# Attention with two expert layers on one core: 64-row tile first, raw float32 scores for it, loads spread over three queues

## The chip, the cores and the metric

One core of a Trainium2 chip runs the whole program. TensorE (PE) multiplies, VectorE (DVE), ScalarE (ACT) and GpSimd (POOL) do the rest, and the sync engine (SP) issues transfers; ACT and POOL can issue transfers too. The metric is the device time of one execution in microseconds, the median of several runs.

## The reference

Two batches of 8 heads, 576 positions, 64 numbers per head. A learned bias depends on the positions alone. The result goes through two layers of experts.

```python
scores = q @ k.T / sqrt(64)
bias = relu(x @ w1 + b1) @ w2        # x = log1p(|i - j|) / log1p(max(i, 1)), 32 hidden, 8 heads
attn = softmax(scores + bias);  y = attn @ v
y = sum_e p[:, e] * (relu(y @ w1[e]) @ w2[e])    # 4 experts, given probabilities
y = sum_e P[:, e] * (relu(y @ w1[e]) @ w2[e])    # 8 experts, P from 8 Sinkhorn rounds
```

## The kernel before

**Attention** takes the first 200 us or so. Rows of the scores are cut into tiles t = 0 to 3 of 128 rows for each batch, and a tile t = 4 that holds the last 64 rows of both batches. Heads go in pairs p = 0 to 3. A unit is one (t, p, b), or one (4, p): 36 units, in the order of `tps_` (t = 0, 4, 1, 2, 3). Units are numbered 0 to 35, and k is the pass of the loop that starts unit k.

A pass issues, in this order, for the units in flight: the scores of unit k (`emit_S`, TensorE, into two PSUM tiles tagged `sc`), for which q and k were first split into a rounded part and a rest (`prep_q`, `prep_k`: three products instead of one); score plus bias with the row minimum of the negative (`emit_max`, DVE, one instruction for each head); `emit_recip2` of unit k-1; `emit_x` of unit k-4 (DVE: divides the product with V and writes `rows`); the two exponentials (`emit_exp`, ACT); the transposes of unit k-2 (`emit_T`, TensorE) and their copies out (`emit_evac`, ACT); one more group of the bias; and the product with V of unit k-3 (`emit_P`, TensorE, into `po`). Every engine runs its own instructions in the order in which they were issued; there is no scheduler.

**The bias** of 16 rows is a group, 36 in all. Hidden values come from DVE or ACT (`emit_hid`), TensorE multiplies (`bps`), ACT copies out into one of three staging slots (`bsts`, two instructions), and the sync queue stores to memory (`bd`). `load_bias` reads a unit pair's bias back (`bt`, two buffers); it waits until the groups of its tile are stored. For tile 4 it takes four transfers. Tile 4 has another head pair in each unit, the other tiles in every second unit. Eleven groups are made before the loop, one in each pass after it.

**Queues.** All transfers before are on the sync queue in one order: q (`qr`), k (`kr`), V, the bias both ways, later the weights.

**The rest.** From unit 15 on, finished rows are cut up for the first expert layer (`pieces`: ACT copies, then DVE), one part in a pass. The expert layers follow, with TensorE busy nearly throughout.

Of the kernel before, what the change touches and what calls it, by code (L numbers as in the profile page):

```python
# [9 lines left out]
F32 = mybir.dt.float32  # L10
# [38 lines left out]
def attn_moe_moe(ctx: ExitStack, tc: tile.TileContext, pack, keep, rel, qT, kT, vT, w, out):  # L49
# [126 lines left out]
    def attention(moe):  # L176
# [19 lines left out]
        def load_v(p):  # L196
            sy.dma_start(out=V[p][:, 0:4, :], in_=vT[p, 0:512].rearrange("(j p) x -> p j x", p=128))
            gp.memset(V[p][:, 4, :], 0.0)
            for h in range(2):
                to, of = (x.rearrange("p (b h d) -> p h b d", b=2, h=2)[:, h] for x in (V[p][:, 4, :], vT[p, 512:576]))  # L200
                sy.dma_start(out=to[64 * h:64 * h + 64], in_=of)

        bdram = [dram.tile([H, (128 if t < 4 else 64) + 1, W], F32, name=f"bd{t}") for t in range(5)]


        tps_ = [(t, p) for t in (0, 4, 1, 2, 3) for p in range(4)]
        units = [(t, p, b) for t, p in tps_ for b in range(2 if t < 4 else 1)]
# [3 lines left out]

        def load_k(p, b):
            i = 2 * p + b
            r = xa.tile([128, 1280], F32, tag=f"x0{XA[i % 4]}", name=f"kr{p}{b}")[:, 0:S]
            for h in range(2):
                sy.dma_start(out=r[64 * h:64 * h + 64], in_=kT[p, b, 0:64, S * h:S * h + S])
            rawk[p, b] = r

        def prep_k(p, b, hi):
            r = rawk.pop((p, b))  # L220
            kk[p, b] = ata.tile([128, 2, S], F32R, name=f"kk{p}{b}")
            h = kk[p, b][:, 0, :]
            if hi is sc:
                sc.activation(out=h, in_=r, func=AF.Copy)
            else:
                ve.tensor_copy(h, r)
            ve.tensor_tensor(out=kk[p, b][:, 1, :], in0=r, in1=h.bitcast(F32), op=ALU.subtract)

        def load_q(t, p):
            r = ata.tile([128, 256], F32, tag="qraw", name=f"qr{t}{p}", bufs=3)  # L230
            for h in range(2):
                sy.dma_start(
                    out=r[64 * h:64 * h + 64].rearrange("p (b c) -> p b c", b=2),
                    in_=qT[t, p, 0:64].rearrange("p (b h c) -> p h b c", b=2, h=2)[:, h],
                )
            rawq[t, p] = r

        def prep_q(t, p):
            r = rawq.pop((t, p))
# [30 lines left out]
        taken = {}  # L270
        MORE = 56

# [64 lines left out]
        def emit_S(u):  # L337
            t, p, b = units[u]
            o = [ps.tile([128, 2, 512], F32, tag="sc", name=f"sc{u}{h}", bufs=2) for h in range(2)]

            todo = [(x, y, bb) for x, y in ((0, 1), (1, 0), (0, 0)) for bb in ([b] if t < 4 else [0, 1])]
            for j in range(2):
                for i, (x, y, bb) in enumerate(todo):
                    for h in range(2):
                        d = slice(64 * h, 64 * h + 64)
                        pe.matmul(  # L346
                            out=o[h][:, j, 0:288],
                            lhsT=qq[t, p][d, x, 128 * bb:128 * bb + 128],
                            rhs=kk[p, bb][d, y, 288 * j:288 * j + 288],
                            start=i == 0,  # L350
                            stop=i == len(todo) - 1,
                        )
# [134 lines left out]

        FIRST = 8
        hids(8, (1, 5))
        for g in range(FIRST):  # L490
            groups(1)
            if g == 0:
                prep_q(*tps_[0])
            if g == 1:
                prep_k(*kq[0], ve)
            hids(4, (1,))
            if g == 3:
                load_k(*kq[3])
            if g == 4:
                prep_k(*kq[1], ve)  # L500
            if g == 6:
                load_k(*kq[4])
                load_q(*tps_[2])

        load_bias(*tps_[0])
        load_bias(*tps_[1])
        load_k(*kq[5])
        load_q(*tps_[3])
        prep_q(*tps_[1])
        prep_k(*kq[2], sc)  # L510
        for _ in range(3):
            groups(1)
            hids(4)
        prep_k(*kq[3], sc)

        ti, work, first_split = 0, [], None
        for k in range(U + 3):
            first = False
            if k < U:
                t, p, b = units[k]  # L520
                first = b == 0
                if first:
                    ti = tps_.index((t, p))
# [30 lines left out]
            hids(2)  # L554
            if k >= 3 and k - 3 < U:
# [428 lines left out]
```

## Time and profile before

| | us |
|---|---|
| median of 3 runs (1386.51 to 1392.95) | 1389.74 |
| the profiled execution | 1390.56 |
| its span, first to last instruction | 1388.6 |
| start of the first score reduction | 29.8 |
| start of that of unit 12 | 95.3 |
| start of that of unit 35 (the last) | 198.8 |

Times in the views count from the span's start. "Idle before, releaser" in square brackets is how long an engine stood still before an instruction and what ended it. PE busy is modelled. Matmuls of float32 leave two records each, of the rounded type one.

### The profile page before, as it was taken

The page shows a single profiled execution, that of the slowest core. Times are in us where ns is not written, and L with a number is a line of the kernel's source. Part 1 is how long each engine was busy: PE and PEld are TensorE (multiplying, and loading weights), DVE is VectorE, ACT ScalarE, POOL GpSimd, SP SyncE. Part 2 cuts the span into 40 slices and gives each one's busy share as a digit, 9 for nine tenths or more (in the row PEclk, how much of TensorE's full clock was granted, in tenths as well). Part 3 has the DMA queues.
Part 4 walks back from the last instruction along what each step waited for, and adds up shares of the span by engine and source line. Part 5 has one row for each costly group of instructions (what it writes and reads, how often), then busy time and mean ns, then how long its engine had stood idle before and what let it go on. Part 6 is the DMA issues. An engine that isn't in the chain of part 4 may idle for free.

```text
span 1388.6 us, 22435 instructions
## 1 busy us (share of the span) xinstructions
PE 1343.7 (97%) x8763; PEld 1172.5 (84%) x8763; DVE 794.9 (57%) x1786; ACT 507.1 (37%) x1208; POOL 390.4 (28%) x391
## 2 busy tenths in 40 slices
PE   7889988999999999999999999999999999999998
PEld 3666676899899898889888898898998988988987
DVE  7768778456464473584585463563554744735643
ACT  6768774233142241344242241331321422413311
POOL 0111134044062160153061160350430612604400
PEclk9999999999999999999999999999999999999999
DMA  7765521111021020011021030020110200301110
GB/s 211 197 175 145 156 66 61 31 58 65 0 85 38 1 95 27 1 61 61 1 91 31 3 96 24 31 92 1 62 61 1 92 31 24 96 4 33 59 39 31
DMA packets 42169, 84.67 MB, mean 61 GB/s; under 512 B 10320, under 2 KB 17744, under 8 KB 42064
## 3 DMA queue, kind: packets, MB, share of 16 engines
q1 hardware_dynamic: 42064, 83.24, 19.6%
q8 instruction: 69, 1.13, 0.3%
q14 instruction: 36, 0.29, 0.1%
HBM read 69.97 MB, written 13.25 MB: 60 GB/s over the span
## 4 chain that ended last, share of the span: by engine, by line
PE 84%; DVE 8%; ACT 3%; DMA 2%; issue 2%; SPq 1%; POOL 0%; DVEq 0%; ACTq 0%; POOLq 0%
PE y L726 42%; PE B L647 16%; PE C L647 10%; PE A L647 10%; DVE s L364 2%; PE po L435 2%; PE sc L346 1%; ACT s L377 1%; DMA bt<-bd 1%; DMA bd<-bsts 1%; PE bps L297 1%; PE tp L409 1%; ACT bsts L326 1%; ACT at L418 1%; DVE wt L158 0%
## 5 line engine op out<-in xcount | busy, mean ns | idle before, releaser
L726 PE MATMUL y<-gb,h 128*128 128x512 f32 x2592 | 717.3, 397 | 0.0
L726 PEld LDWEIGHTS y<-gb,h 128*128 128x128 f32 x2592 | 454.1, 189 | 57.0 <-issue 0.2
L162 POOL TENSOR_TENSOR gb<-rawb,gb 128x512 fp32r<-128x512 f32 x94 | 126.1, 1354 | 644.1 <-ACT gb L161 611.6
L655 DVE TENSOR_TENSOR u<-B,s 128x320 f32<-128x320 f32 (+1 forms) x192 | 87.7, 457 | 309.9 <-PE B L647 309.9
L658 ACT ACTIVATE h<-c 128x320 fp32r<-128x320 f32 (+1 forms) x288 | 119.9, 439 | 390.6 <-DVE c L655 389.2
L661 DVE SCALAR_TENSOR_TENSOR h<-c,h 128x320 fp32r<-128x320 f32 (+1 forms) x288 | 172.0, 614 | 48.3 <-ACT h L658 43.8
L655 DVE TENSOR_TENSOR c<-C,u 128x320 f32<-128x320 f32 (+1 forms) x192 | 87.5, 456 | 60.9 <-PE C L647 57.5
L162 POOL TENSOR_TENSOR ga<-rawa,ga 128x512 fp32r<-128x512 f32 x94 | 120.9, 1305 | 4.5 <-ACT ga L161 4.5
L162 POOL TENSOR_TENSOR ga<-wt,ga 128x512 fp32r<-128x512 f32 x94 | 106.0, 1147 | 35.5 <-ACT ga L161 17.9
L669 ACT ACTIVATE s<-A 128x320 f32<-128x320 f32 (+1 forms) x96 | 39.4, 411 | 177.5 <-PE A L647 177.4
L658 ACT ACTIVATE h<-A 128x320 fp32r<-128x320 f32 (+1 forms) x96 | 39.0, 406 | 147.0 <-PE A L647 146.7
L655 DVE TENSOR_TENSOR c<-B,s 128x320 f32<-128x320 f32 (+1 forms) x96 | 44.0, 458 | 81.5 <-PE B L647 80.2
L161 ACT ACTIVATE gb<-rawb 128x512 fp32r<-128x512 f32 x96 | 60.1, 627 | 80.7 <-DMA rawb<-in_w 80.7
L377 ACT ACTIVATE s<-s,stat 128x576 f32<-128x576 f32 x72 | 55.4, 769 | 42.4 <-DVE stat L364 41.6
L435 PEld LDWEIGHTS po<-at,V 128*64 128x64 f32 x800 | 39.3, 137 | 33.9 <-DVE rows L445 32.7
L647 PE MATMUL A<-x20A,ga 128*128 128x320 f32 x384 | 66.9, 309 | 0.0
L647 PE MATMUL B<-x20S,ga 128*128 128x320 f32 x384 | 66.8, 309 | 0.0
L647 PE MATMUL C<-x20S,ga 128*128 128x320 f32 x384 | 66.7, 309 | 0.0
L647 PEld LDWEIGHTS B<-x20S,ga 128*128 128x128 f32 x384 | 61.6, 188 | 5.8
L647 PEld LDWEIGHTS A<-x20A,ga 128*128 128x128 f32 x384 | 61.5, 188 | 5.7
L647 PEld LDWEIGHTS C<-x20S,ga 128*128 128x128 f32 x384 | 61.3, 188 | 5.8
L435 PE MATMUL po<-at,V 128*64 128x128 f32 (+1 forms) x800 | 47.5, 267 | 16.3 <-DVE rows L445 16.3
(167 smaller groups left out, 1905.9 us busy)
## 6 DMA issues: line engine op xcount, KB each, us to landing
rawa<-in_w SPq DMA_DIRECT2D x48, 512.0 KB, 4.0
rawb<-in_w SPq DMA_DIRECT2D x48, 512.0 KB, 4.9
bd<-bsts SPq DMA_DIRECT2D x36, 295.5 KB, 3.4
bt<-bd SPq DMA_DIRECT2D x16, 512.0 KB, 4.4
qr<-in_qT SPq DMA_DIRECT2D x40, 64.0 KB, 3.2
kr<-in_kT SPq DMA_DIRECT2D x16, 144.0 KB, 3.3
V<-in_vT SPq DMA_DIRECT2D x4, 512.0 KB, 4.7
bt<-bd SPq DMA_DIRECT2D x8, 256.0 KB, 4.1
```

Source lines behind the costliest of these rows:

```text
L161: sc.activation(out=z(0), in_=src, func=AF.Copy)
L162: lo.tensor_tensor(out=z(1), in0=src, in1=z(0).bitcast(F32), op=ALU.subtract)
L297: pe.matmul(out=o[32 * q:32 * q + 32, j, 0:n], lhsT=w2n, rhs=hid[g, q][:, n * j:n * j + n], start=True, stop=True,)
L364: ve.tensor_tensor_reduce(out=s.rearrange("p (a j) -> p a j", a=2), in0=scps.pop((u, h))[:, :, 0:288], in1=bt[t, p][:, S * h:S * h + S].re ...
L377: sc.activation(out=s, in_=s, func=AF.Exp, scale=-1.0, bias=stat[u][:, h:h + 1], accum_out=stat[u][:, 2 + h:3 + h],)
L435: pe.matmul(out=o[64 * h:64 * h + 64, c0:c0 + n], lhsT=V[p][:, j, col:col + D], rhs=rhs, start=j == 0, stop=j == 4,)
L647: pe.matmul(out=ban[o], lhsT=a, rhs=x[:, z, k, :], start=not more and i == 0, stop=i == 5, skip_group_check=more,)
L655: ve.tensor_tensor(out=t[o], in0=ban[a], in1=t[b], op=ALU.add)
L658: sc.activation(out=h[f][:, 0, half, :], in_=src, func=AF.Relu)
L661: ve.scalar_tensor_tensor(out=h[f][:, 1, half, :], in0=src, scalar=0.0, in1=h[f][:, 0, half, :].bitcast(F32), op0=ALU.max, op1=ALU.subtract,)
L669: sc.activation(out=t["s1"], in_=ban["A"], func=AF.Copy)
L726: pe.matmul(out=self.y[t], lhsT=a, rhs=x, start=g == 0 and f == 0 and i == 0, stop=g == NP - 1 and f == 1 and i == 2,)
```

## The change

- `tps_` begins with tile 4: its four units are 0 to 3, tile 0's are 4 to 11. From unit 12 on the units are the same. The groups are made in the order 32 to 35, then 0 to 31; nine stand before the loop.
- Tile 4's scores are taken in float32 from raw q and k: 8 matmuls of 64 rows by 64 columns by 288 instead of 24.
- k of a head pair comes as one tile for both batches, all four from ACT's queue at the start. `prep_k` stands in passes 1 to 8, all with ACT.
- q and V come through GpSimd's queue, q three pairs ahead instead of four.
- `emit_x` stands before `emit_S` and `emit_max` of its pass, no longer behind them.
- Six matmuls on ones stand behind the scores in passes 0 to 2. Pass 4 makes two groups; pass 3 makes four more hidden rows.

```diff
-            sy.dma_start(out=V[p][:, 0:4, :], in_=vT[p, 0:512].rearrange("(j p) x -> p j x", p=128))
+            gp.dma_start(out=V[p][:, 0:4, :], in_=vT[p, 0:512].rearrange("(j p) x -> p j x", p=128))
...
-        tps_ = [(t, p) for t in (0, 4, 1, 2, 3) for p in range(4)]
+        tps_ = [(t, p) for t in (4, 0, 1, 2, 3) for p in range(4)]
-        def load_k(p, b):
+        def load_k(p, eng):
+            for b in range(2):
+                rawk[p, b] = r[:, S * b:S * b + S]
             for h in range(2):
-                sy.dma_start(out=r[64 * h:64 * h + 64], in_=kT[p, b, 0:64, S * h:S * h + S])
+                eng.dma_start(
+                    out=r[64 * h:64 * h + 64, 0:2 * S].rearrange("d (b s) -> d b s", b=2),
+                    in_=kT[p, :, 0:64, S * h:S * h + S].rearrange("b d s -> d b s"),
+                )
-            r = ata.tile([128, 256], F32, tag="qraw", name=f"qr{t}{p}", bufs=3)
+            r = ata.tile([128, 256], F32, tag="qraw", name=f"qr{t}{p}", bufs=4)
             for h in range(2):
-                sy.dma_start(
+                gp.dma_start(
...
-            todo = [(x, y, bb) for x, y in ((0, 1), (1, 0), (0, 0)) for bb in ([b] if t < 4 else [0, 1])]
+            todo = [(b, 0, 128, x, y) for x, y in ((0, 1), (1, 0), (0, 0))] if t < 4 else [(0, 0, 64, None, None), (1, 64, 64, None, None)]
...
+                        a, m = (qq[t, p][:, x], kk[p, bb][:, y]) if t < 4 else (rawq[t, p], rawk[p, bb])
                         pe.matmul(
-                            out=o[h][:, j, 0:288],
+                            out=o[h][c:c + n, j, 0:288],
...
+        def busy(n):
+            for _ in range(n):
+                pe.matmul(out=po_all[:, 0, 0:128], lhsT=ones, rhs=ones, start=True, stop=True)
...
+        for p in range(4):
+            load_k(p, sc)
+        for i in range(3):
+            load_q(*tps_[i])
-        order = list(range(8)) + list(range(32, NGR)) + list(range(8, 32))
+        order = list(range(32, NGR)) + list(range(32))
-        FIRST = 8
+        FIRST = 4
...
+        load_bias(*tps_[0])
+        load_v(0)
+        for g in range(5):
+            groups(1)
+            hids(4, (1,))
             if g == 0:
+                load_bias(*tps_[1])
+            if g == 2:
+                load_v(1)
...
+                if k >= 4:
+                    emit_x(k - 4)
                 emit_S(k)
+                if k < 3:
+                    busy(6)
                 emit_max(k)
                 if k > 0:
                     emit_recip2(k - 1)
-                if k >= 4:
-                    emit_x(k - 4)
...
-            groups(1)
+            groups(2 if k == 4 else 1)
...
-            if k < 4:
-                prep_k(*kq[k + 4], sc)
+            if 0 < k < 9:
+                prep_k(*kq[k - 1], sc)
             if k < 2:
-                load_k(*kq[k + 6])
-            if k < 8 and k % 2 == 0:
-                load_v(k // 2)
+                load_v(k + 2)
```

The order on three queues, in places that matter below.

DVE around the fifth unit before (`kk31` is the rest of k for pair 3, batch 1; `s4` the reduced scores of unit 4; `rows0` what `emit_x` writes):

```order
L387 RECIPROCAL stat2_467<-stat2_467 128x2
L283 TENSOR_SCALAR hids_109<-T_99,b1psi_98 128x384 x2
L227 TENSOR_TENSOR kk31_583<-kr31_448,kk31_583 128x576
L364 ISA s4_603,stat4_602<-sc40_586,bt02_442 128x576
L364 ISA stat4_602 128x1
L364 ISA s4_603,stat4_602<-sc41_587,bt02_442 128x576
L364 ISA stat4_602 128x1
L387 RECIPROCAL stat3_534<-stat3_534 128x2
L445 TENSOR_TENSOR rows0_76<-po_95,at02_488 128x128
```

and around the seventh unit now:

```order
L286 TENSOR_SCALAR hidS3_156<-T_99,b1psi_98 128x368 x2
L286 TENSOR_SCALAR hidS4_157<-T_99,b1psi_98 128x368 x2
L230 TENSOR_TENSOR kk20_742<-kr2_130,kk20_742 128x576
L449 TENSOR_TENSOR rows4_80<-po_95,at22_610 128x128
L368 ISA s6_763,stat6_762<-sc60_746,bt01_566 128x576
L368 ISA stat6_762 128x1
L368 ISA s6_763,stat6_762<-sc61_747,bt01_566 128x576
L368 ISA stat6_762 128x1
L391 RECIPROCAL stat5_681<-stat5_681 128x2
L286 TENSOR_SCALAR hids_109<-T_99,b1psi_98 128x352 x4
```

A `kk` row stands ahead of the reduction in both, now with `rows4`, the `emit_x` of unit 2, between them; before, `rows0` stood behind the reduction. Such a `kk` row stands ahead of the reduction of units 2 to 9 now, and stood ahead of units 1 to 4 in the loop before.

The sync queue from the store of group 32 on before (`bd` is a store of a bias group, `bt` a load):

```order
L329 DMA bd4_108<-bsts_110 16x8x591 x4
L232 DMA qr40_393<-in_qT 64x2x128 x2
L216 DMA kr30_399<-in_kT 64x576 x2
L197 DMA V0_100<-in_vT 128x4x256
L201 DMA V0_100<-in_vT 64x2x64 x2
L329 DMA bd1_105<-bsts_110 16x8x591
L255 DMA bt02_442<-bd0_104 128x2x512
L256 DMA bt02_442<-bd0_104 128x2x64
L216 DMA kr31_448<-in_kT 64x576 x2
L329 DMA bd1_105<-bsts_110 16x8x591
L232 DMA qr41_508<-in_qT 64x2x128 x2
L197 DMA V1_101<-in_vT 128x4x256
```

and now:

```order
L332 DMA bd4_108<-bsts_110 16x8x591 x4
L258 DMA bt40_224<-bd4_108 64x2x512
L259 DMA bt40_224<-bd4_108 64x2x64
L258 DMA bt40_224<-bd4_108 64x2x512
L259 DMA bt40_224<-bd4_108 64x2x64
L332 DMA bd0_104<-bsts_110 16x8x591
L258 DMA bt41_249<-bd4_108 64x2x512
L259 DMA bt41_249<-bd4_108 64x2x64
L258 DMA bt41_249<-bd4_108 64x2x512
L259 DMA bt41_249<-bd4_108 64x2x64
L332 DMA bd0_104<-bsts_110 16x8x591 x5
L258 DMA bt42_356<-bd4_108 64x2x512
```

The loads of q, k and V have gone from between the stores and the loads of the bias. Tile 4's loads, four for each unit, stand ahead of the store of tile 0's first group, and the second unit's ahead of that of the next five.

GpSimd's own order in the first passes before (`stat` readies the denominators of a unit, `spread` writes their reciprocals out wide):

```order
L383 TENSOR_SCALAR stat0_367<-stat0_367 128x2
L198 MEMSET V0_100 128x256
L389 COPY spread0_425<-stat0_367 128x128
L383 TENSOR_SCALAR stat1_420<-stat1_420 128x2
L389 COPY spread1_472<-stat1_420 128x128
L383 TENSOR_SCALAR stat2_467<-stat2_467 128x2
```

and now:

```order
L387 TENSOR_SCALAR stat0_334<-stat0_334 128x2
L235 DMA qr43_353<-in_qT 64x2x128 x2
L197 DMA V2_102<-in_vT 128x4x256
L198 MEMSET V2_102 128x256
L201 DMA V2_102<-in_vT 64x2x64 x2
L393 COPY spread0_386<-stat0_334 128x128
L387 TENSOR_SCALAR stat1_381<-stat1_381 128x2
L235 DMA qr00_403<-in_qT 64x2x128 x2
L197 DMA V3_103<-in_vT 128x4x256
L198 MEMSET V3_103 128x256
L201 DMA V3_103<-in_vT 64x2x64 x2
L393 COPY spread1_441<-stat1_381 128x128
L387 TENSOR_SCALAR stat2_436<-stat2_436 128x2
```

Five transfers stand between `stat0` and `spread0`, and five more between `stat1` and `spread1`.

## Rows read from the trace of the kernel before

**Rows 1.** The page: span, and busy time of each engine.

```profile
span 1388.6 us, 22435 instructions
PE 1343.7 (97%) x8763; PEld 1172.5 (84%) x8763; DVE 794.9 (57%) x1786; ACT 507.1 (37%) x1208; POOL 390.4 (28%) x391
```

**Rows 2.** Busy time of PE, PEld, DVE, ACT, POOL by stretch; then clock, DMA.

```profile
0.00:95.30 95.30, 79.35 (x790) 52.38 (x790) 66.39 (x192) 64.40 (x141) 9.18 (x32) 0.95 0.73 200
95.30:201.80 106.50, 93.78 (x1143) 72.76 (x1143) 84.60 (x271) 84.31 (x223) 25.72 (x63) 1.00 0.47 131
```

**Rows 3.** DVE in order of time (start, us, instruction): first score reduction of nine units.

```profile
29.77 0.76 DVE L364 CUSTOM_DVE_ANT_0 s<-sc,bt 128x576 f32<-128x576 f32 x1 [1.60 <-DMA bt<-bd]
...
41.29 0.75 DVE L364 CUSTOM_DVE_ANT_0 s<-sc,bt 128x576 f32<-128x576 f32 x1
...
53.05 0.75 DVE L364 CUSTOM_DVE_ANT_0 s<-sc,bt 128x576 f32<-128x576 f32 x1
...
57.30 0.76 DVE L364 CUSTOM_DVE_ANT_0 s<-sc,bt 128x576 f32<-128x576 f32 x1 [0.47 <-PE sc L346]
...
76.69 0.76 DVE L364 CUSTOM_DVE_ANT_0 s<-sc,bt 128x576 f32<-128x576 f32 x1 [0.95 <-PE sc L398]
...
95.31 0.76 DVE L364 CUSTOM_DVE_ANT_0 s<-sc,bt 128x576 f32<-128x576 f32 x1 [2.86 <-DMA bt<-bd]
...
156.10 0.75 DVE L364 CUSTOM_DVE_ANT_0 s<-sc,bt 128x576 f32<-128x576 f32 x1
...
160.18 0.76 DVE L364 CUSTOM_DVE_ANT_0 s<-sc,bt 128x576 f32<-128x576 f32 x1
...
190.24 0.76 DVE L364 CUSTOM_DVE_ANT_0 s<-sc,bt 128x576 f32<-128x576 f32 x1 [1.06 <-PE sc L346]
```

**Rows 4.** The chain of waits in order of time, 0 to 110 us (start, us, what).

```profile
1.15 3.39 DMA T<-in_rel
...
22.38 3.24 DMA bd<-bsts
...
42.09 0.70 ACT s L377
...
45.89 0.58 ACT kk L224
46.49 0.76 DVE kk L227
...
84.77 3.68 DMA bt<-bd
```

**Rows 5.** The chain of waits, 150 to 200 us.

```profile
161.70 0.20 DVE rows L445
...
161.94 1.31 PE po L435 x20
163.26 1.03 PE sc L346 x12
```

**Rows 6.** ScalarE (ACT) in order of time, first 10 us.

```profile
0.71 1.28 ACT L285 ACT_TABLE_LOAD   x1 [0.71 <-PEq L973]
5.12 1.43 ACT L285 ACTIVATE hids<-T,b1psi 128x576 f32<-128x576 f32 x2 [3.13 <-DVE T L466]
7.82 1.05 ACT L326 ACTIVATE bsts<-bps,cst 128x576 f32<-128x576 f32 x2 [1.27 <-PE bps L297]
...
9.40 1.04 ACT L326 ACTIVATE bsts<-bps,cst 128x560 f32<-128x560 f32 x2
```

**Rows 7.** The sync queue (SPq), in order of time.

```profile
1.62 1.31 SPq L232 DMA_DIRECT2D qr<-in_qT  x2
...
62.15 0.60 SPq L255 DMA_DIRECT2D bt<-bd  x1
```

**Rows 8.** Who waited for whom (us, times, longest), 0 to 210 us.

```profile
PE po L435 <- DVE rows L445: 16.3, 18, 2.2
```

**Rows 9.** The page's costliest groups: one GpSimd (POOL) operation.

```profile
L162 POOL TENSOR_TENSOR gb<-rawb,gb 128x512 fp32r<-128x512 f32 x94 | 126.1, 1354 | 644.1 <-ACT gb L161 611.6
```

More of the change, by code (lines that the diff above doesn't have):

```diff
@@ L200, in load_v @@
                 to, of = (x.rearrange("p (b h d) -> p h b d", b=2, h=2)[:, h] for x in (V[p][:, 4, :], vT[p, 512:576]))
-                sy.dma_start(out=to[64 * h:64 * h + 64], in_=of)
+                gp.dma_start(out=to[64 * h:64 * h + 64], in_=of)
         bdram = [dram.tile([H, (128 if t < 4 else 64) + 1, W], F32, name=f"bd{t}") for t in range(5)]
-        tps_ = [(t, p) for t in (0, 4, 1, 2, 3) for p in range(4)]
+        tps_ = [(t, p) for t in (4, 0, 1, 2, 3) for p in range(4)]
         units = [(t, p, b) for t, p in tps_ for b in range(2 if t < 4 else 1)]
@@ L209, in attention @@
         kk, qq, bt, rawk, rawq = {}, {}, {}, {}, {}
-        def load_k(p, b):
-            i = 2 * p + b
-            r = xa.tile([128, 1280], F32, tag=f"x0{XA[i % 4]}", name=f"kr{p}{b}")[:, 0:S]
+        def load_k(p, eng):
+            r = xa.tile([128, 1280], F32, tag=f"x0{XA[p]}", name=f"kr{p}")
+            for b in range(2):
+                rawk[p, b] = r[:, S * b:S * b + S]
             for h in range(2):
-                sy.dma_start(out=r[64 * h:64 * h + 64], in_=kT[p, b, 0:64, S * h:S * h + S])
-            rawk[p, b] = r
+                eng.dma_start(
+                    out=r[64 * h:64 * h + 64, 0:2 * S].rearrange("d (b s) -> d b s", b=2),
+                    in_=kT[p, :, 0:64, S * h:S * h + S].rearrange("b d s -> d b s"),
+                )
         def prep_k(p, b, hi):
-            r = rawk.pop((p, b))
+            r = rawk[p, b]
             kk[p, b] = ata.tile([128, 2, S], F32R, name=f"kk{p}{b}")
@@ L238, in prep_q @@
         def prep_q(t, p):
-            r = rawq.pop((t, p))
+            r = rawq[t, p]
             a = ata.tile([128, 2, 256], F32R, tag="qq", name=f"qq{t}{p}", bufs=3)
@@ L270, in attention @@
         taken = {}
-        MORE = 56
+        MORE = 76
         def emit_hid(g, eng, q):
@@ L339, in emit_S @@
             o = [ps.tile([128, 2, 512], F32, tag="sc", name=f"sc{u}{h}", bufs=2) for h in range(2)]
-            todo = [(x, y, bb) for x, y in ((0, 1), (1, 0), (0, 0)) for bb in ([b] if t < 4 else [0, 1])]
+            todo = [(b, 0, 128, x, y) for x, y in ((0, 1), (1, 0), (0, 0))] if t < 4 else [(0, 0, 64, None, None), (1, 64, 64, None, None)]
             for j in range(2):
-                for i, (x, y, bb) in enumerate(todo):
+                for i, (bb, c, n, x, y) in enumerate(todo):
                     for h in range(2):
                         d = slice(64 * h, 64 * h + 64)
+                        a, m = (qq[t, p][:, x], kk[p, bb][:, y]) if t < 4 else (rawq[t, p], rawk[p, bb])
                         pe.matmul(
-                            out=o[h][:, j, 0:288],
[L348 to L351, printed above, removed]
+                            out=o[h][c:c + n, j, 0:288],
+                            lhsT=a[d, 128 * bb + c:128 * bb + c + n],
+                            rhs=m[d, 288 * j:288 * j + 288],
+                            start=t == 4 or i == 0,
+                            stop=t == 4 or i == len(todo) - 1,
                         )
@@ L453, in attention @@
         gp.memset(ones, 1.0)
-        for _ in range(WARM):
-            pe.matmul(out=po_all[:, 0, 0:128], lhsT=ones, rhs=ones, start=True, stop=True)
+        def busy(n):
+            for _ in range(n):
+                pe.matmul(out=po_all[:, 0, 0:128], lhsT=ones, rhs=ones, start=True, stop=True)
+        busy(WARM)
         sy.dma_start(out=cst, in_=pack)
         sy.dma_start(out=T, in_=rel)
-        load_q(*tps_[0])
-        load_k(*kq[0])
-        load_k(*kq[1])
+        for p in range(4):
+            load_k(p, sc)
+        for i in range(3):
+            load_q(*tps_[i])
         sy.dma_start(out=kept, in_=keep)
-        load_q(*tps_[1])
-        load_k(*kq[2])
         ve.tensor_scalar(b1psi, cst[:, C_PSI:C_PSI + 144], b1col, None, op0=ALU.mult)
@@ L491, in attention @@
             groups(1)
-            if g == 0:
[L493 to L511, printed above, removed]
-            groups(1)
-            hids(4)
-        prep_k(*kq[3], sc)
+            hids(4, (1,))
[3 more added lines that the diff above has]
+            groups(1)
+            hids(4, (1,))
+            if g == 0:
+                load_bias(*tps_[1])
+            if g == 2:
+                load_v(1)
         ti, work, first_split = 0, [], None
@@ L547, in attention @@
                 emit_evac(k - 2, 2, sc)
-            groups(1)
+            groups(2 if k == 4 else 1)
             if k >= 2 and k - 2 < U:
@@ L553, in attention @@
                 emit_recip(k)
-            hids(2)
+            hids(6 if k == 3 else 2)
             if k >= 3 and k - 3 < U:
@@ L560, in attention @@
             if first:
-                if ti + 2 < len(tps_):
+                if 4 <= ti + 2 < len(tps_):
                     prep_q(*tps_[ti + 2])
-                if ti + 4 < len(tps_):
-                    load_q(*tps_[ti + 4])
+                if ti + 3 < len(tps_):
+                    load_q(*tps_[ti + 3])
             last = t == 4 or b == 1
```

## The prediction

> **What bounds the kernel now.** I read the page's head first, then busy time by stretch, then the chain of waits of the first 200 us, then DVE, ACT and the sync queue in order of time there. TensorE is busy for 97% of the span [rows 1], so little is to be had outside attention. The change touches the first 202 us. There no engine is full: TensorE is busy for 79 of 95 us in the first twelve units and 94 of 106 in the rest, DVE and ACT for about 70% and 80% [rows 2]. So what counts is the loop of waits that sets the distance from one unit's score reduction on DVE to the next. I call the start of that reduction M(k). Read from [rows 3], M(0) is 29.77, M(2) 41.29, M(4) 53.05, M(5) 57.30, M(9) 76.69, M(12) 95.31, M(25) 156.10, M(26) 160.18 and M(33) 190.24. Three regimes are to be seen:
>
> - Units 2 to 4 are 5.88 us apart, (53.05 - 41.29) / 2. The chain shows why [rows 4]: ACT does its list of unit 2 without a gap from 42.09 to 46.47, and the list ends with the rounding of k (45.89); DVE takes the rest of k (46.49) and only then the next reduction, which releases ACT's next list. It is one loop over two engines.
> - Units without such a rounding are 4.25 apart (57.30 - 53.05), set by TensorE.
> - From unit 9 to unit 12, three units take 18.62. These read tile 4's bias, four transfers for each unit, and wait for it.
>
> Late in attention (from unit 16 on) the parts of `pieces` put the first kind of loop back in many passes.
>
> **The change, part by part.**
>
> *Start.* T lands at 4.54 as before (1.15 + 3.39 [rows 4]), or later, since k now comes beside it. ACT had its table at 2.0 and began its hidden rows at 5.12 [rows 6]. Now eight issues of k stand ahead of the table. The last waits for a semaphore that T's landing frees, so ACT is ready at 4.5 + 0.6 for an issue [rows 7] + 1.3 for the table = 6.4. The first copy-out moves from 7.82 to about 9.1, and groups follow at 1.6 each (9.40 - 7.82 [rows 6]). The fourth ends at 14.9; its store takes 3.24 to land [rows 4] after an issue delay of about 0.1, at 18.2. The sync queue then issues four loads of unit 0's bias (0.60 each [rows 7], to 20.6) and only behind them the store of the fifth group, then four loads for unit 1 (to 23.6), then the store of the sixth. The eighth copy-out reuses the fifth's staging slot, so it waits to 23.8; the ninth waits for the sixth's landing at 26.8. With the hidden row behind it, ACT reaches unit 0's exponentials at about 28.5. Two exponentials take 1.6 (0.70 and a read each [rows 4]), the tenth copy-out 1.0 [rows 6]; its store is issued to 31.8, unit 2's four loads start to 33.6 and land 3.68 later [rows 4]. So M(2) is about 37.4. I take 38.0, since TensorE may run part of this at the lower clock. Against 41.29 that is -3.3. The other end is 41.7, if the clock is low through units 0 and 1.
>
> *All eight roundings of k in the loop.* Passes 1 to 8 end ACT's list with one, where passes 2 and 3 had one before. So the 5.88 loop runs from M(2) to M(9). In passes from the fourth on `emit_x` also stands between the rest of k and the reduction, 0.20 [rows 5], 6.07 a unit. Pass 4 has a second group, 1.04 of ACT [rows 6]. M(9) - M(2) = 5.88 + 6.07 + 7.1 + 4 x 6.07 = 43.3; before 76.69 - 41.29 = 35.4. That is +7.9. Less than this cannot come out while ACT and DVE keep their order.
>
> *Tile 4's bias waits gone from units 8 to 12.* M(12) - M(9) becomes 3 x 4.3 = 12.9 against 18.62: -5.7. Together with the start M(12) moves by -1.1 only: what the early scores win is handed back to the roundings.
>
> *`emit_x` ahead of the reduction, later units.* In some ten units from 16 on the reduction follows DVE work that waits for ACT; each gets 0.19 longer, +1.9. In pass 32 DVE waited 1.06 for scores [rows 3], which waited for a V product that waited for `emit_x`; there about 0.9 comes back. Net +1.0. Where TensorE sets the pace, nothing changes. The ends are -1.0 and +2.5.
>
> *The last group comes one pass later.* Two fewer groups are made ahead of the loop and pass 4 makes up one. M(26) - M(25) was 4.08 [rows 3] without a group; with one it is about 1.0 longer (the copy-out, 1.04 [rows 6]). +1.0.
>
> *Transfers on GpSimd's queue.* Five stand between `stat0` and `spread0`, and five between `stat1` and `spread1`. TensorE transposes `spread` of unit k-2 right behind the scores of unit k, and that unit's reduction waits for it. No row shows a transfer issued by GpSimd. The nearest below is the sync queue's 0.60 [rows 7]: then `spread0` is ready at 30.1 + 0.5 + 5 x 0.6 + 0.6 = 34.2, ahead of unit 2's bias, cost 0. The nearest above is GpSimd's tensor operation of 1.35 [rows 9]: `spread0` at 38.0, `spread1` at 38.0 + 0.6 + 6.8 + 0.6 = 46.0 against M(3) at 43.9, cost 2.5 with the transposes. At 2.0 each `spread1` is at 52.5 and the cost is 9. I take +1.0, between the first two.
>
> The Trainium skill speaks against this part: "SBUF — State Buffer", section "A bandwidth-pool intuition that's wrong", and the warning above it say that a transfer issued by GpSimd has its descriptors written by GpSimd and waits while DVE holds the port they share, about 620 ns alone and 3100 ns beside a DVE copy. By 3.1 each, `spread1` would come at 63, the cost would be some 20 us and the time about 1411. DVE has no such work all the time, so I hold that for an upper end that nothing here shows; it is part of the first rival's chance.
>
> *Hidden elsewhere.* Tile 4's float32 scores have 16 records in place of 24, and the warm-up matmuls (ten took 4.63 us at the start) stand where TensorE waits anyway; in the first two units they could delay it, and that is in the 41.7 above. With q off the sync queue each bias load of tile 4 stands 1.31 earlier behind its store [rows 7], which is in the chain above.
>
> *Sum.* -3.3 + 7.9 - 5.7 + 1.0 + 1.0 + 1.0 = +1.9 on the profiled execution's 1390.56: 1392.4. That run is 0.8 above the median of the runs, so I forecast 1392 as a median (1391.6, rounded up).
>
> **The rivals.**
>
> - *GpSimd's issue is slow.* From 2 us for each transfer on, `spread1` sets M(3); at 2.0 the time is 1392 - 1 + 9 = 1400. For it: ten transfers in two passes on a queue that others wait for. Against: GpSimd is idle there (9 us busy of 95 [rows 2]), and its transfers of q need only be there a unit later.
> - *`emit_x` was the brake.* TensorE stood still for 16.3 us in 18 waits before V products, all for `emit_x` [rows 8]; the chain runs through them (161.70, 161.94, 163.26 [rows 5]). If that idle time is worth its length, the time is 1392 - 1.0 - 16.3 = 1375; if half, 1383. Against: the row of M(26) has no idle time before it [rows 3], so the next limit, DVE's own work behind ACT's, is right behind the one removed.
> - *A cold start.* TensorE at the lower clock through units 0 and 1 makes M(2) 41.7 in place of 38.0: 1396.
> - *The roundings hide*, because DVE gets to the reduction first. Then M(9) is M(2) + 7 x 4.3 and the time 1392 - 13 = 1379. The order on DVE excludes it.
>
> **How the numbers follow.** Forecast 0.60, with its own range from 1388 to 1397. Slow issue on GpSimd 0.15, `emit_x` as the brake 0.11, cold start 0.13, hidden roundings 0.01. The range from 1384 to 1400 leaves out most of the brake and the slow issue from 2.0 us up. Half a percent is 7 us, about what a measurement of this kernel can tell from no change: faster means under 1382.8, slower over 1396.7. Faster 0.11 (the brake, mostly), slower 0.25 (slow issue, half of the cold start, the top of the forecast), the same 0.64.
>
> **What would show it.** M(2) between 37 and 39, with ACT's eighth and ninth copy-outs waiting for stores. Distances of 5.9 to 6.1 in seven units after it, and near 7 behind unit 4; M(12) within 2 of 95.3. No wait of DVE for `bt` from unit 8 on. TensorE's wait for `emit_x` nearly gone, and distances late in attention unchanged or 0.2 longer. Distances near 4.4 in units 4 to 8 would prove me wrong, as would M(12) under 90, or GpSimd's issues above 1.5 us with DVE waiting for the transposes of `spread`.

## Result, and the profile after

The change makes the kernel slower: 1406.39 us (median of 4 runs, 1403.15 to 1409.67) against 1390.4 (the runs of 1389.74 with one more), a ratio of 1.0111 with a 95% interval of 1.0096 to 1.0125. The forecast was 1392 with a range from 1384 to 1400, so it missed, on the slow side. The profiled execution of after took 1403.15 us. Its page answers to [rows 1]:

```profile
span 1401.3 us, 22451 instructions
PE 1349.1 (96%) x8767; PEld 1171.7 (84%) x8767; DVE 789.6 (56%) x1774; ACT 508.8 (36%) x1212; POOL 422.9 (30%) x443
```

TensorE's busy time grew by 5 us and the span by 12.7. Where those are is read as in [rows 3], from DVE in order of time; these are the score reductions of units 2, 3, 4, 5, 9 and 12:

```profile
52.42 0.76 DVE L368 CUSTOM_DVE_ANT_0 s<-sc,bt 128x576 f32<-128x576 f32 x1 [6.33 <-DMA bt<-bd]
...
58.77 0.76 DVE L368 CUSTOM_DVE_ANT_0 s<-sc,bt 128x576 f32<-128x576 f32 x1 [0.39 <-DMA bt<-bd]
...
64.98 0.75 DVE L368 CUSTOM_DVE_ANT_0 s<-sc,bt 128x576 f32<-128x576 f32 x1
...
73.97 0.74 DVE L368 CUSTOM_DVE_ANT_0 s<-sc,bt 128x576 f32<-128x576 f32 x1
...
99.29 0.75 DVE L368 CUSTOM_DVE_ANT_0 s<-sc,bt 128x576 f32<-128x576 f32 x1
...
112.07 0.76 DVE L368 CUSTOM_DVE_ANT_0 s<-sc,bt 128x576 f32<-128x576 f32 x1 [0.64 <-PE sc L350]
```

M(2) is 52.42 where 38.0 was forecast: 14.4 late before the loop has settled. M(9) - M(2) is 46.87 (forecast 43.3), M(12) - M(9) 12.78 (12.9). From M(12) to M(35) the trace has 105.71 where it had 103.47 before. Behind M(35) the profiled execution is 6.3 shorter than before's; the code there is the same, and over the profiles of all kernels below that stretch scatters from 1183.5 (after itself) to 1191.3 us, so single profiles are compared by M(k) and the kernels by their medians and ratios.

The chain of waits of after, 0 to 60 us, shows what the start consists of:

```profile
0.74 6.36 DMA kr<-in_kT
...
9.07 1.28 ACT L288
...
13.22 0.32 ACT bsts L329
...
14.29 7.95 DMA bd<-bsts
...
22.33 0.28 ACT bsts L329
...
29.18 4.42 DMA bd<-bsts
...
33.69 0.71 ACT bsts L329
...
34.78 2.19 PE sc L350 x14
36.98 2.06 PE po L461 x12
39.04 0.97 PE bps L300 x8
...
43.68 0.67 ACT bsts L329
...
48.47 10.14 DMA bt<-bd
```

Four transfers stand in it. The stores take 7.95 and 4.42 where 3.24 was the price [rows 4], the bias load of unit 3 takes 10.14 for 3.68 [rows 4], and ACT's table load, at 0.71 before [rows 6], comes at 9.07, behind eight issues of k of which the last three wait for the first to land (6.36). M(2) itself waits for unit 2's four loads; the DMA view from 41.5 to 44.6 us, when they are issued, has

```profile
bt<-bd SPq DMA_DIRECT2D x2, 256.0 KB, 7.2
...
bt<-bd SPq DMA_DIRECT2D x2, 32.0 KB, 8.3
```

The DMA view of the first 60 us says that this is no matter of more bytes. Before (the line of packets, then issues with KB each and the median us to landing):

```profile
DMA packets 9662, 12.16 MB, mean 203 GB/s; under 512 B 2520, under 2 KB 5432, under 8 KB 9656
...
kr<-in_kT SPq DMA_DIRECT2D x16, 144.0 KB, 3.3
...
V<-in_vT SPq DMA_DIRECT2D x3, 512.0 KB, 4.6
...
T<-in_rel SPq DMA_DIRECT2D x1, 288.0 KB, 3.4
```

and after:

```profile
DMA packets 6836, 12.05 MB, mean 201 GB/s; under 512 B 2032, under 2 KB 2288, under 8 KB 6832
...
kr<-in_kT ACTq DMA_DIRECT2D x8, 288.0 KB, 11.2
V<-in_vT POOLq DMA_DIRECT2D x4, 512.0 KB, 10.6
...
T<-in_rel SPq DMA_DIRECT2D x1, 288.0 KB, 6.3
```

12 MB at 200 GB/s in both. But before, six units' reductions had begun by then (M(5) 57.30), and after, four (M(3) 58.77): all of k and half of V are issued in the first 14 us, and T, the stores and the bias loads run among them.

### The profile page after: what moved, and what is told of

Its sections match the earlier page's. It is cut to its first block, busy times and chain, and to the rows that moved or that the text cites. A ratio compares the mean times of both kernels' runs of the same rounds, so it can differ in the third digit from the quotient of the medians.

```text
span 1401.3 us, 22451 instructions
## 1 busy us (share of the span) xinstructions
PE 1349.1 (96%) x8767; PEld 1171.7 (84%) x8767; DVE 789.6 (56%) x1774; ACT 508.8 (36%) x1212; POOL 422.9 (30%) x443
## 4 chain that ended last, share of the span: by engine, by line
PE 84%; DVE 7%; ACT 6%; DMA 2%; issue 1%; ACTq 0%; SPq 0%; POOL 0%; DVEq 0%; POOLq 0%
PE y L721 41%; PE B L642 16%; PE A L642 10%; PE C L642 10%; ACT s L381 2%; ACT at L422 1%; PE bps L300 1%; PE sc L350 1%; ACT bsts L329 1%; PE po L439 1%; DMA bd<-bsts 1%; DVE s L368 1%; PE tp L413 1%; DMA bt<-bd 1%; DMA kr<-in_kT 0%
## 5 line engine op out<-in xcount | busy, mean ns | idle before, releaser
L656 DVE SCALAR_TENSOR_TENSOR h<-c,h 128x320 fp32r<-128x320 f32 (+1 forms) x288 | 166.4, 594 | 48.8 <-ACT h L653 44.0
L368 DVE CUSTOM_DVE_ANT_0 s<-sc,bt 128x576 f32<-128x576 f32 x72 | 51.4, 750 | 20.7 <-PE sc L350 13.7
L642 PEld LDWEIGHTS B<-x21S,ga 128*128 128x128 f32 x384 | 54.4, 188 | 5.9
## 6 DMA issues: line engine op xcount, KB each, us to landing
V<-in_vT POOLq DMA_DIRECT2D x4, 512.0 KB, 10.6
```

The lines of the kernel that those rows point to most:

```text
L368: ve.tensor_tensor_reduce(out=s.rearrange("p (a j) -> p a j", a=2), in0=scps.pop((u, h))[:, :, 0:288], in1=bt[t, p][:, S * h:S * h + S].re ...
L642: pe.matmul(out=ban[o], lhsT=a, rhs=x[:, z, k, :], start=not more and i == 0, stop=i == 5, skip_group_check=more,)
L656: ve.scalar_tensor_tensor(out=h[f][:, 1, half, :], in0=src, scalar=0.0, in1=h[f][:, 0, half, :].bitcast(F32), op0=ALU.max, op1=ALU.subtract,)
```

## The experiments

All are edits of the changed kernel or of the one before. M(k) is read from DVE's order of time, one profile for each kernel; the ratio is against the kernel before. The runs of before that went with them have medians from 1389.1 to 1392.4 (e5 to e8 the lowest, e13 to e15 the highest), so kernels of different groups are better compared by ratios. How far M(k) can be trusted shows in e8: up to pass 4 it is the same program as after, and its M(0) is 2.6 and its M(2) 1.9 earlier. Differences of 2 to 3 us at one M(k) of the start say little by themselves.

| kernel | M(0) | M(2) | M(5) | M(9) | M(12) | M(35) | median us | ratio, 95% interval |
|---|---|---|---|---|---|---|---|---|
| before | 29.77 | 41.29 | 57.30 | 76.69 | 95.31 | 198.78 | 1390.4 | |
| after | 37.02 | 52.42 | 73.97 | 99.29 | 112.07 | 217.78 | 1406.39 | 1.0111 [1.0096, 1.0125] |
| e1 V late | 32.82 | 44.69 | 67.30 | 92.64 | 105.42 | 211.19 | 1403.21 | 1.0081 [1.0066, 1.0097] |
| e2 k in parts | 32.07 | 46.52 | 68.10 | 93.44 | 106.22 | 211.75 | 1404.52 | 1.0096 [1.0074, 1.0119] |
| e3 both | 31.98 | 43.59 | 67.27 | 92.62 | 105.40 | 210.91 | 1401.82 | 1.0070 [1.0049, 1.0091] |
| e4 one queue | 34.22 | 46.96 | 70.48 | 95.84 | 108.62 | 214.15 | 1404.94 | 1.0100 [1.0083, 1.0117] |
| e5 e3, no warm-up | 32.76 | 45.11 | 67.01 | 92.37 | 105.17 | 210.67 | 1403.75 | 1.0100 [1.0080, 1.0120] |
| e6 e3, no V | 31.59 | 43.84 | 66.00 | 91.32 | 104.11 | 209.57 | 1402.93 | 1.0104 [1.0080, 1.0128] |
| e7 k on DVE | 35.55 | 51.48 | 71.46 | 90.89 | 103.68 | 209.16 | 1399.81 | 1.0081 [1.0058, 1.0105] |
| e8 product back | 34.44 | 50.54 | 70.39 | 94.93 | 107.71 | 212.65 | 1407.16 | 1.0132 [1.0109, 1.0154] |
| e9 e3+e7+e8 | 33.25 | 45.32 | 69.80 | 89.11 | 101.89 | 206.57 | 1397.37 | 1.0052 [1.0033, 1.0070] |
| e10 e9, stores first | 30.67 | 41.89 | 64.37 | 83.70 | 96.48 | 201.17 | 1394.83 | 1.0019 [1.0007, 1.0032] |
| e11 before, k on DVE | 29.48 | 41.45 | 54.66 | 74.31 | 92.16 | 195.88 | 1388.49 | 0.9975 [0.9965, 0.9984] |
| e12 before, queues split | 31.13 | 42.29 | 58.30 | 77.98 | 94.12 | 197.74 | 1390.21 | 0.9995 [0.9985, 1.0004] |
| e13 no bytes of k, V | 31.27 | 43.75 | 65.58 | 90.94 | 103.72 | 209.26 | 1399.07 | 1.0048 [1.0034, 1.0061] |
| e14 e11, q and V split | 29.92 | 41.08 | 54.28 | 73.59 | 90.75 | 194.38 | 1386.33 | 0.9960 [0.9948, 0.9973] |
| e15 e14, bias early | 29.24 | 40.74 | 53.95 | 72.72 | 88.83 | 192.48 | 1385.28 | 0.9951 [0.9937, 0.9964] |

**The theory:** the start is late because transfers that nothing paces (little in their own queues holds them back) run beside the urgent ones. Rivals: TensorE's lower clock; the order of stores and loads on the sync queue.

*e1*, V later:

```diff
-        load_v(0)
-            if g == 2:
-                load_v(1)
-            if k < 2:
-                load_v(k + 2)
+            if 0 < k < 5:
+                load_v(k - 1)
```

> The changed kernel, with the twelve loads of V taken out of the first 45 us of GpSimd's queue and issued in passes 1 to 4 instead. Theory (what is late is the data: transfers of k, q and V that nothing paces run beside T, the bias stores and the bias loads): the first bias store lands in about 5 us and not 7.95, unit 2's bias loads in 4 to 5 and not 8.5, unit 2's score reduction starts near 44 and not 52.4, time near 1398. Rival (TensorE at the lower clock is what makes the start late): the start moves by under 2 us, time 1404 to 1407. Rival (the order on the sync queue, tile 4's loads ahead of the later stores): as the second, under 2 us.

*e2*, k in parts:

```diff
-        for p in range(4):
-            load_k(p, sc)
+        load_k(0, sc)
...
+            if g % 2 == 0:
+                load_k(1 + g // 2, sc)
...
+                load_k(3, sc)
```

> The changed kernel, with only head pair 0's k loaded at the start; pairs 1 and 2 are issued by ScalarE behind the copy-outs of the first and third group, pair 3 behind unit 1's bias loads. Theory (unpaced transfers delay the data): T lands at about 4.6 and not 7.46, ScalarE's first copy-out starts near 9.5 and not 14, but V still runs beside the stores: unit 2's score reduction near 48, time near 1402. Rival (cold clock) and rival (order on the sync queue): T comes earlier but the reduction of unit 2 stays within 2 us of 52.4, time 1404 to 1407.

*e3* is both edits. *e4* has one queue again, q and V likewise:

```diff
-            load_k(p, sc)
+            load_k(p, sy)
...
-            gp.dma_start(out=V[p][:, 0:4, :], ...)
+            sy.dma_start(out=V[p][:, 0:4, :], ...)
```

> Both of these edits: V late and k in parts. Theory (unpaced transfers delay the data): unit 2's score reduction comes to 39 to 40, where the forecast had it, and the time to about 1393. Rivals (cold clock; order on the sync queue): unit 2 stays over 49, time over 1402. If the two edits help by the sum of what each gives alone, the backlog is the sum of both; if by less, one of them hides the other.

> The changed kernel with the three queues put back into one: k, q, V and bias all issued by the sync queue, in the changed kernel's order; the tile order, float32 scores, roundings and the place of the output product stay. Theory (the queues running together delay the urgent transfers): T lands near 4.6, unit 2's score reduction starts between 42 and 45 (the queue's own issue time now stands ahead of the stores), time near 1397. Rival (cold clock or the order of stores and loads): unit 2 stays near 52, time 1404 or more.

M(2) moved as the theory said in e1 (44.69 for "near 44") and e2 (46.52 for "near 48"), far beyond the rivals' 2 us. The two gains, 7.7 and 5.9, come to 8.8 together and not 13.6, which fits one backlog cut from two sides. But e3 stopped at 43.59, not at 39 to 40, and none of these medians fell by what M(2) did (e3: 4.6 us, 5.7 by the ratios); the times of e1 and e2 are nearer the rivals' (1403.21 for 1398, 1404.52 for 1402). One queue alone (e4) gave 5.5 at M(2) and nothing in the time that can be told. Its DMA view of the first 60 us:

```profile
bd<-bsts SPq DMA_DIRECT2D x13, 295.5 KB, 3.7
...
T<-in_rel SPq DMA_DIRECT2D x1, 288.0 KB, 3.3
```

With the program order of after but a single queue, T is back at its price, and the stores nearly (a median of 3.7 for after's 4.5); now the first store, whose data are ready at 8.6, is issued at 14.69, behind k's landing (8.28 in the chain). So transfers in the way are a cause, and not the only one.

On top of e3, *e5* drops the warm-up matmuls of the passes, and *e6* V's loads (all three loads of a pair, as in e13; the cuts show one):

```diff
-                if k < 3:
-                    busy(6)
```

```diff
-            gp.dma_start(out=V[p][:, 0:4, :], ...)
+            gp.memset(V[p][:, 0:4, :], 0.0)
```

> V late and k in parts, and in addition without the six warm-up matmuls in each of the first three passes (the ten ahead of the loop stay). Theory A (the 36 records of passes 0 to 2 stand on the path, ahead of the bias products that ScalarE waits for: 1.99 + 1.53 us in the trace of the run with both edits): unit 2's score reduction 3 earlier, at 40 to 41, time near 1399. Theory B (they hold TensorE at the higher clock and their place is free): the reduction of unit 2 where it was, 43.6, and units 3 to 5 longer at the lower clock, time 1402 to 1405.

> V late and k in parts, and V not read at all (zeros in its place, so this kernel leaves the V product's data out; its matmuls stay). Theory (the DMA engines are full until unit 5 or so, 0.8 to 0.9 busy at about 215 GB/s, and V's 2.4 MB stand in that stretch): unit 3's bias lands in about 4 us and not 8.05, unit 3's reduction starts near 48 and not 50.9, pass 4 takes 7.1 to 7.5 and not 9.85 since TensorE no longer stands still for a store and does not fall to the lower clock; unit 9's start near 87 and not 92.6; time near 1396. Rival (the chain of copy-outs and stores alone sets it): under 2 us.

Theory A of e5 was wrong; of B the time came true, and not the longer units (M(2) to M(5) takes 21.9, in e3 23.7). The warm-up matmuls do stand on the path, but without them the same stretch runs at a lower clock. Busy time by stretch, clock as the third figure from the right, e3 and then e5:

```profile
32.00:43.60 11.60, 11.13 (x102) 7.06 (x102) 6.66 (x19) 7.24 (x16) 5.61 (x11) 0.96 0.64 173
```

```profile
32.00:43.60 11.60, 9.63 (x72) 3.12 (x66) 6.68 (x18) 7.19 (x16) 4.41 (x9) 0.68 0.61 169
```

At 0.68 of the full 2.4 GHz part of it ran at 1.2; M(2) is 1.5 later and M(9) 0.3 earlier, both within the scatter, and the time is not to be told apart. In e6, without V's bytes, M(9) is 1.3 earlier, within the scatter too; pass 4 still takes 9.00. What holds e3 is in the chain of waits of *e13*, in which the bytes of V and of three of k's pairs are gone from the start:

```diff
+            if p:
+                for b in range(2):
+                    rawk[p, b] = rawk[0, b]
+                return
...
-            gp.dma_start(out=V[p][:, 0:4, :], ...)
+            gp.memset(V[p][:, 0:4, :], 0.0)
```

> The changed kernel with V and the last three head pairs of k not read (zeros for V, the first pair's k in place of the others, so this kernel computes with wrong data; every matmul, rounding, store and bias load stays). Theory (the bytes of k and V beside T, the stores and the bias loads are the whole loss of the start): T lands near 4.6, the first store in about 3.3, unit 2's reduction between 38 and 40; passes behind it as forecast, unit 9 at 82 to 85, time 1391 to 1394. Rival (the order of stores and loads on the sync queue, and the scores' PSUM buffer that waits for a copy-out, keep a part): unit 2 at 42 or later, time over 1395.

```profile
1.18 5.29 DMA T<-in_rel
...
17.34 3.50 DMA bd<-bsts
...
20.86 0.63 SPq L262
...
22.84 0.61 SPq L263
...
23.49 4.37 DMA bd<-bsts
...
31.23 2.86 PE po L465 x12
...
36.45 1.53 PE po L465 x12
```

and in ACT's order of time (the eighth, ninth and tenth copy-out):

```profile
27.94 1.05 ACT L333 ACTIVATE bsts<-bps,cst 128x528 f32<-128x528 f32 x2 [5.29 <-DMA bd<-bsts]
...
31.21 1.05 ACT L333 ACTIVATE bsts<-bps,cst 128x512 f32<-128x512 f32 x2 [1.62 <-DMA bd<-bsts]
...
35.45 1.05 ACT L333 ACTIVATE bsts<-bps,cst 128x496 f32<-128x496 f32 x2 [1.09 <-PE bps L304]
```

The rival was right for the rest: M(2) is 43.75. The path is the forecast's own, link by link, and each link is longer than its price. T still takes 5.29, beside the first pair of k and q, and the fourth copy-out ends at 17.3 for 14.9; its store takes 3.50; the fifth store, issued at 23.49 behind unit 0's loads, takes 4.37 beside these. So ACT's eighth copy-out comes at 27.94 (forecast 23.8) and its ninth at 31.21 (26.8), and the tenth waits 1.09 more for a product behind the warm-up matmuls (2.86 on the chain). From 31.2 to 34.1 the granted clock is 0.50, the lower level; a pass later, at 1.00, the same six matmuls take 1.53, so the lower clock adds 1.33 here, more than the whole wait. Of the 14.4 us, 8.7 (52.42 - 43.75) go with the bytes of k and V, and with six issues fewer on ACT; 5.8 do not. The time of e13 fell with it, by 8.8 by the ratios (7.3 in the medians).

*e7* rounds k on DVE alone, *e8* moves the output product back:

```diff
-                prep_k(*kq[k - 1], sc)
+                prep_k(*kq[k - 1], ve)
```

```diff
-                if k >= 4:
-                    emit_x(k - 4)
                 emit_S(k)
...
                 if k > 0:
                     emit_recip2(k - 1)
+                if k >= 4:
+                    emit_x(k - 4)
```

> The changed kernel with both halves of k's rounding on VectorE in passes 1 to 8; nothing else differs. Theory (one loop over ScalarE and VectorE sets 6.14 us in these passes): VectorE no longer waits for ScalarE's rounding; its own list is about 4.8 us long, so the distances of units 6 to 8 fall from 6.14 to about 4.8, unit 9 comes about 6 to 9 earlier against unit 2, time near 1399. Rival (TensorE or the transfers set these distances): they stay over 5.9, time 1404 to 1407.

> The changed kernel with the output product back behind the score reduction, as before the change. By the forecast (+1.0 of the sum): unit 12 to unit 35 takes 103.5 to 105 and not 105.7, time 1 us less, within what can be told from none. Rival (the output product was the brake before, and moving it saved TensorE's waits): the time rises by 5 us or more.

In e7 units 5 to 9 start at

```profile
71.46 0.76 DVE L368 CUSTOM_DVE_ANT_0 s<-sc,bt 128x576 f32<-128x576 f32 x1 [0.61 <-PE sc L350]
...
75.81 0.76 DVE L368 CUSTOM_DVE_ANT_0 s<-sc,bt 128x576 f32<-128x576 f32 x1 [0.17 <-PE sc L350]
...
80.56 0.75 DVE L368 CUSTOM_DVE_ANT_0 s<-sc,bt 128x576 f32<-128x576 f32 x1
...
84.81 0.76 DVE L368 CUSTOM_DVE_ANT_0 s<-sc,bt 128x576 f32<-128x576 f32 x1
...
90.89 0.75 DVE L368 CUSTOM_DVE_ANT_0 s<-sc,bt 128x576 f32<-128x576 f32 x1
```

4.35, 4.75 and 4.25 apart where it was 6.13 each: the loop over two engines is shown, and M(9) - M(2) falls by 7.5. In e8 the distances are 0.2 shorter (5.94 for 6.13) and M(12) to M(35) 104.94 for 105.71. The time rose by 0.8 in the medians and 2.9 by the ratios, whose intervals overlap, so it does not settle the rival at 5 us alone. The waits do (0 to 210 us, as [rows 8]), here of after:

```profile
PE po L439 <- DVE rows L449: 1.5, 4, 0.8
```

The change took away nearly all of TensorE's 16.3 us of waiting for `emit_x`, e8 brings it back (16.3 in 17 waits), and M(12) to M(35) is no shorter without it. That idle time was worth nothing.

*e9* is e3, e7 and e8 together. *e10* adds:

```diff
-        load_bias(*tps_[0])
         for g in range(5):
...
-            if g == 0:
-                load_bias(*tps_[1])
+            if g == 1:
+                load_bias(*tps_[0])
                 load_k(3, sc)
+            if g == 2:
+                load_bias(*tps_[1])
```

> V late, k in parts, k's rounding on VectorE, and the output product behind the reduction, all in the changed kernel. Theory (start and roundings are two separate losses, in series): unit 2's reduction near 43.5 as with the two load edits, unit 2 to unit 9 near 38.5, unit 9 near 82, unit 35 near 199.5 against 198.8 before; time 1389 to 1392. Rival (what one edit frees is taken back by the other, as V's edit and k's took from each other): unit 35 over 203, time over 1394.

> The same with the first two bias loads moved on the sync queue: unit 0's behind the stores of the fifth and sixth group, unit 1's behind that of the seventh (k's last pair with unit 0's). Theory (ScalarE stood still in the start because the fifth group's store waited on the sync queue behind unit 0's loads, which wait for the fourth store to land): its copy-outs of the eighth and ninth group come 3 to 4 earlier, unit 0's scores with them; unit 2's reduction near 40, time near 1387. Rival (the DMA engines are full in that stretch, 0.86 busy, so the order does not matter): unit 2 stays within 1 of the run before it, and so the time.

e9 missed (1397.37 for 1389 to 1392): M(9) - M(2) is 43.8, not 38.5, since in passes 2 to 4 (7.40, 7.12 and 9.96) the roundings were not the only limit. In e10 the eighth and ninth copy-out start at 24.83 and 26.36 (e9: 29.92 and 33.69), as the theory had it; M(2) is 3.4 earlier (45.32 to 41.89), M(12) 5.4, and the time fell by 2.5 (4.6 by the ratios) to 1394.83, far from the 1387 expected. The longest wait left in the start of e10 is one bias load of tile 4, in the chain and in the busy time by stretch (DMA share and GB/s are the last two figures):

```profile
41.10 8.31 DMA bt<-bd
```

```profile
41.00:48.00 7.00, 4.57 (x31) 2.18 (x31) 4.71 (x13) 3.77 (x9) 3.26 (x8) 0.83 0.96 209
```

Here the DMA engines are full. With tile 4 first, the first four units need all of k, all of V and four bias loads of 576 KB; with tile 0 first, the first four units needed half of each.

*e11* and *e12* go the other way, from the kernel before: k's roundings of the loop on DVE, or the queues alone split, each transfer in its place (q as V):

```diff
-                prep_k(*kq[k + 4], sc)
+                prep_k(*kq[k + 4], ve)
```

```diff
-                sy.dma_start(out=r[64 * h:64 * h + 64], in_=kT[...])
+                sc.dma_start(out=r[64 * h:64 * h + 64], in_=kT[...])
...
-            sy.dma_start(out=V[p][:, 0:4, :], ...)
+            gp.dma_start(out=V[p][:, 0:4, :], ...)
```

> The kernel before, with the four roundings of k in passes 0 to 3 on VectorE alone. Theory (the loop over both engines holds on this side as well): the distances behind units 2 and 3 fall from 5.88 to 4.3 to 4.8, unit 5's reduction comes 2 to 3 earlier than 57.3; from unit 8 on tile 4's bias waits take part of it back. Unit 12 near 93 to 95, time 1387 to 1390. Rival: distances stay at 5.9.

> The kernel before, with only the queues changed: k issued by ScalarE, q and V by GpSimd, each where it stands in the program. Theory (the loss of the change's start is that transfers run together, and here program order still paces k): T lands within 0.5 of 4.5; unit 2's reduction moves by 0 to +3, mostly from ScalarE's own issue time (0.63 for each of six transfers ahead of its table); time 1390 to 1394. Rival (the split by itself is the loss): unit 2 over 46, time over 1396.

e11 is faster than before, as expected. e12 is the clearest cut: the split of the queues, with program order still pacing k and V, costs nothing in the time. T takes 4.2 there and M(2) is 1.0 later, and M(12) - M(9) falls from 18.62 to 16.14. The Trainium skill ("DMA: Bandwidth & Descriptors", section "Issuing engines are not separate DMA queues") says that transfers from several engines run interleaved on the same 16 DMA engines, and that issuing from several saves only issue time. e12 agrees; after's T, 6.3 us for 3.4, shows the other side of it.

*e14* is e11 with e12's edit for q and V (not for k). *e15* adds to it a third bias buffer and earlier bias loads:

```diff
-        x = ata.tile([128, 2 * 640], F32, tag="bt", name=f"bt{t}{p}", bufs=2)
+        x = ata.tile([128, 2 * 640], F32, tag="bt", name=f"bt{t}{p}", bufs=3)
...
-            if k < U and last and ti + 2 < len(tps_):
-                load_bias(*tps_[ti + 2])
+            if k < U and first and ti + 2 < len(tps_) and tps_[ti + 2][0] != 4:
+                load_bias(*tps_[ti + 2])
+            if k < U and last and ti + 3 < len(tps_) and tps_[ti + 3][0] == 4:
+                load_bias(*tps_[ti + 3])
```

> The kernel before, with k's rounding in the loop on VectorE and q and V issued by GpSimd; k stays on the sync queue. Theory (the two gains are at different places and add): start as before, unit 5 near 54.6, unit 9 to unit 12 in 16.1 and not 18.6, unit 12 near 90.5, time near 1386.5. Rival (tile 4's waits take the gain back): as with the rounding alone, 1388.5.

> The same with a third bias buffer, and bias loads issued one pass earlier (those of tile 4 one tile and head pair earlier). Theory (the waits of units 8 to 12 are the latency of a load that is issued only two units ahead): unit 9 to unit 12 in 13 to 14, unit 12 near 88, time 1383 to 1385. Rival (the DMA engines' volume: each unit of tile 4 moves as many bias bytes as two of another tile): 15.5 to 16.5, time as without.

Both are faster than before and after. e14 met its time, though M(12) - M(9) is 17.16, not 16.1. In e15 the rival was right for the stretch (16.11); whether bytes or latency hold it was not separated. Its time is not to be told from e14's.

## Why the prediction was wrong

- **The step that failed is *Start*,** "T lands at 4.54 as before", and with it "so ACT is ready at" 6.4, "its store takes 3.24 to land" and "land 3.68 later". The text named k as running beside T, gave that no price, and said nothing of k, q and V beside the stores and loads; it priced each from rows of a kernel in which one queue issued everything, so that they had few neighbours. Measured: T 6.3, stores 7.95 and 4.42, unit 2's loads 7.2 and 8.3 (medians). ACT was ready at 10.35, as its last three issues of k waited for k's own first landing and not for T. Along the path the delay grows so: first copy-out 13.22 for 9.1 (+4.1), end of the fourth, which waits for the first store, 23.38 for 14.9 (+8.5), ninth 37.21 for 26.8 (+10.4), M(2) 52.42 for 38.0 (+14.4). About 4 us each are ACT's queue, the first store and unit 2's loads.
- **What the edits say of these 14.4,** good to 2 or 3 us: 8.7 go with the bytes of k and V at the start and the six issues of k on ACT (e13, which does not part them). The other 5.8 are the same links without them: 2.4 up to the fourth copy-out (T alone 1.9), 1.7 to the eighth (the two stores and the issues between), 1.1 at the tenth's product, the rest 0.5. A part of this is the order on the sync queue, which the forecast followed rightly and priced too low; with the stores ahead, 3.4 came back (e10 against e9).
- **The cold start** was a rival at 0.13. Stretches of the start do run at the lower level, and in e13 this accounts for the 1.1 at the tenth's product. That is a small part of the 14.4, and e5 shows no net gain or loss from the warm-up matmuls.
- **The eight roundings** were right as a mechanism (e7) and low in size: 46.87 for 43.3. More than half is pass 4, 8.99 for 7.1. The chain of waits there:

```profile
68.20 0.52 ACT bsts L329
...
68.75 0.40 ACT bsts L329
...
69.19 1.74 PE bps L300 x8
...
70.95 0.62 ACT bsts L329
```

  The forecast counted 1.04 of ACT for the second group. Its product also stands on the path, 1.74, because both groups share one PSUM bank and the second waits for the first copy-out. A part of the 1.74 is again the clock: from 69 to 71 us it is 0.50, after TensorE had stood still for 2.9; the next pass's product takes 0.88. Pass 8 took 6.92 for 6.07, as DVE has four extra small operations there.
- **Tile 4's bias waits gone:** right, 12.78 for 12.9.
- **`emit_x` and the last group:** +1.9 and -0.9 and +1.0 were forecast, and M(12) to M(35) rose by 2.2. The parts are where they were put: M(26) - M(25) is 5.20 for 4.08, M(33) - M(32) 2.94 for 4.10 (the forecast's "pass 32" is unit 33), and e8 gives 0.8 back.
- **GpSimd's issue:** costed +1.0, really 0: M(2) and M(3) waited for bias loads, not for `spread`. GpSimd in order of time, after:

```profile
1.29 3.74 POOL L235 DMA_DIRECT2D qr<-in_qT  x6 [0.35 <-issue]
5.02 0.80 POOL L197 DMA_DIRECT2D V<-in_vT  x1
```

  0.62 for each of q's, as on the sync queue. The rule of the Trainium skill that spoke of 3100 ns beside DVE ("SBUF — State Buffer", section "A bandwidth-pool intuition that's wrong") is not seen in these issue times, which run while DVE works. But until 49 us DVE ran sums and reductions and no plain copy, which is what the page's number stands beside, so it is not tested here; what the rule means for the landing (V 10.6 us here, 5.7 in e12) was not separated from the crowd of other transfers.
- **The sum:** M(35) was forecast at 200.7 and is 217.78. Of the 17.1, start +14.4, roundings +3.6, GpSimd -1.0, the rest +0.1. The median is 14.4 over the forecast; the difference lies behind attention, within the scatter there.

## What to carry over

A transfer's latency in a trace belongs to the traffic that ran beside it. Before pricing a start by such rows, add up the bytes due by each deadline, divide by the rate that the trace shows in that stretch (here 200 to 250 GB/s), and see which queue nothing paces. No run here tested that sum as a forecast. And where two pieces of work share one buffer, the second one's whole round trip stands on the path, not its engine time alone.

## What was not expected

Splitting the issue over three queues costs no time when each transfer keeps its place in the program (ratio 0.9995), and delays the urgent transfers twofold to threefold when the queues run ahead (T 6.3 for 3.4, the first store 7.95 for 3.24). And single profiles scatter by some 8 us behind attention: at M(35) e3 and e10 are 6.9 and 16.6 ahead of after, in the medians 4.6 and 11.6. The profiled execution of after has the shortest such stretch of all and is 3.2 under its own median. A step is read at its place in the trace, its worth from the medians and ratios.
